# Halves of the output projection between the values products of the last eight heads: an order forced on TensorE, and a left operand split in its own place

## The chip, the cores and the metric

The kernel runs on one core of one Trainium2 chip. The metric is the device time of one execution in microseconds (us). The engines are named as in the profile: PE is TensorE (matmuls; PEld are its weight loads), DVE is VectorE, ACT is ScalarE, POOL is GpSimd, SP is SyncE, whose queue issues every DMA of this kernel, in order.

## What is computed

The reference is one transformer block with 2048 tokens of 1024 channels: a modulated layer norm, attention over 32 heads of 32 channels in four segments of 512 tokens, with a memory that is carried from segment to segment, and an MLP over the token axis. What the change touches is the end of the attention and what follows it:

```python
o = concat over heads and segments of  g * a_mem + (1 - g) * softmax(q k^T * scale + mask) v
x = x + ga * (o @ wo)                              # the output projection
h = _layernorm(x) * (1 + cb) + sb
x = x + gb * _B_ref(h, w1, b1, w2, b2)             # layer norm again, then the token MLP
```

All of it is in float32. Products of float32 are made of parts: an operand is split into a high part and the rest, and three matmuls (high x high, high x rest, rest x high) are summed.

## The kernel before, in words

**Attention.** 32 iterations t run over two passes of two segments each and eight groups of four heads: `its[t] = (pass, group, segment)`. The last two, t = 30 and 31, are group 7 in segments 2 and 3. A head has the number n = 4t + h. The hand-written loop over n (lines 628 to 651) traces the scores of head n, the row maxima of head n + 3, the values of head n - 1, and a quarter of the projections of the iteration two ahead.

- `maxima` (lines 428 to 453): four matmuls into banks s1 (`sx`, `sy`, `sz`), each reduced on DVE with `mask`; for two heads together a transpose (`nmps`) and four small DMAs (`sk<-nt`) that put the negative maxima into the rows of `sk`.
- `scores` (466 to 488): matmuls `a`, exponentials on ACT into `p32`, a triangle cut on POOL (484), a cast on ACT (486), and the rest of the cast in two POOL instructions (488), the last step before the values.
- `values` (490 to 521): 20 matmuls of `ph` and `vp` into the one bank pv (502), then DVE and POOL; after a group's fourth head four transposes (517), a copy and a DMA of 256 KB into `oT` (520).

**Output projection** (`out_proj`, 698 to 749). 16 tiles of 128 tokens, in the order 0, 1, 8, 2, 9, 3, 10, 4, 11, 5, 12, 6, 13, 7, 14, 15. For each tile `oT` is loaded into `otr` (701, one buffer of 512 KB), split by ACT (121) and DVE (124) into `ots` (two buffers), and `x1` is loaded (705, two buffers). Two halves of 512 columns follow, each of 24 matmuls `po` into a bank pj (716; there are two) and a DVE sum with x1 (719). Then x1 is stored (720), and DVE and ACT make the two norms (`modulated`, `normed`). When both tiles k and k + 8 are there, `paired` makes their combinations and, for k under 3, splits seven operands for the MLP (line 124, `bA`); for the others it stores them (745 to 747, `hcd`). The tiles `h2` have three buffers. `wop` are the pages of wo, split long before (593) and loaded (648) into pages that held h for the projections of t = 30 (first half) and t = 31 (second half).

**Memory.** The buffers of the output projection lie where the attention's were: otr and ots on scb, gaw and the raw buffers; x1, h2 and the rest of pool `cw` on `acst` (among it `mask`, `MZ`, `bdg`) and on the weights of the projections.

**The order of the work.** The kernel is traced as one program; a planner then orders each engine's instructions and SP's DMAs by a timeline of its own, with what is traced earlier going first where both are ready. Nothing in the text of the kernel before sets where po stands among the matmuls of the last heads: the planner does.

**The MLP** (`mix`, line 808, `mx`) begins after the last tile's halves and lasts to the end.

Of the kernel before, what the change touches and what calls it, by code (L numbers as in the profile page):

```python
# [7 lines left out]
F32 = mybir.dt.float32  # L8
# [10 lines left out]
P = 128  # L19
# [9 lines left out]
FT = F // P  # L29
LEADP, LEADS, NSK = 8, 3, 8  # L30
XB = 4
NSC = 4
VL = 1
PHB = 2
# [11 lines left out]
def attention_and_mlp(ctx, tc, x, wq, wkv, wo, beta, w1, b1, w2, b2, c, wm_a, wm_b, out):  # L46
# [29 lines left out]
    def bank(tag, bufs, name):  # L76
        return psum.tile([P, 512], F32, tag=tag, bufs=bufs, name=name)
# [39 lines left out]
    def split(dst, src, hi_eng, lo_eng):  # L117

        hi, lo = dst[:, 0], dst[:, 1]
        if hi_eng is A:  # L120
            A.copy(hi, src)  # L121
        else:
            hi_eng.tensor_copy(hi, src)
        lo_eng.tensor_tensor(lo, src, hi.bitcast(F32), op=ALU.subtract)  # L124
# [18 lines left out]
    def new_page(name):  # L143
        return page.tile([P, 2, 512], F32R, tag="page", bufs=16, name=name)
# [345 lines left out]
    def values(t, h):  # L490
        pr, g, seg = its[t]
        d = st[t]
        am, ph = d["am"], d["ph", h]
        pv = bank("pv", 1, f"pv{t}_{h}").rearrange("p (a n) -> p a n", a=4)
        col = {0: lambda i: 128 * i, 1: lambda i: 512 + 128 * (i - 1), 2: lambda i: 1024 + 128 * (i - 2),
               3: lambda i: 896}
        n = 0
        for part, w in ((0, NV), (1, 65)):
            for i in range(4):
                for j in range(i + 1):  # L500
                    o = col[j](i)
                    T.matmul(pv[:, i, 0:w], ph[:, part, o:o + 128], d["vp"][:, j, h, 0:w], start=(n == 0),  # L502
                             stop=(n == 19), skip_group_check=True)
# [12 lines left out]
        for i in range(4):  # L516
            T.transpose(ps[:, 128 * i:128 * i + 128], am[:, i], ident)
# [20 lines left out]
    def mod_rows(lo, hi):  # L538
# [4 lines left out]
        A.copy(row, ps[0:n, 0:128])  # L543
        SY.dma_start(modd.rearrange("a (b n) -> (a b) n", n=P)[lo:hi], row)

    todo = {}

    def plan(n, f, engines=""):
# [79 lines left out]
    for n in range(-LEADS, 4 * NI + VL):  # L628
# [38 lines left out]
    ot_pools = [tc.tile_pool(name=n, bufs=1, reuse_waits="tile") for n in ("otr", "ots")]  # L667
    wr_, ws_ = (q.__enter__() for q in ot_pools)

    gm = {}  # L670

# [22 lines left out]

    bA = [b_tile(b3, 3, q, "bA0") for q in range(NPR)]
    pair_h = {}

    def out_proj(tt):

        r = wr_.tile([P, NK, P], F32, tag="otr", bufs=1, name=f"otr{tt}")  # L700
        SY.dma_start(r, oT[:, :, P * tt:P * tt + P].rearrange("g p n -> p g n"))
# [3 lines left out]
        SY.dma_start(x1, x[P * tt:P * tt + P])  # L705
        h2 = w.tile([P, D], F32, tag="h2", bufs=3, name=f"h2_{tt}")
# [4 lines left out]
        for nh in range(2):  # L711
            ps = bank("pj", 2, f"po{tt}_{nh}")
            n = 0
            for ct in range(NK):
                for i, j in ((0, 0), (0, 1), (1, 0)):
                    T.matmul(ps, os_[:, i, P * ct:P * ct + P], wop[ct, nh][:, j], start=(n == 0), stop=(n == 3 * NK - 1))  # L716
                    n += 1
            c0, c1 = 512 * nh, 512 * nh + 512
            V.tensor_tensor(x1[:, c0:c1], ps, x1[:, c0:c1], op=ALU.add)  # L719
        SY.dma_start(x1d[tt], x1)  # L720

        def modulated():
            mv = ln_stats(w, x1, "b")
# [24 lines left out]

        return modulated, normed, paired

    for tt in [0] + [i for k in range(1, 8) for i in (k, 7 + k)] + [15]:
        rest = out_proj(tt)
        if tt < 15:
            for f in rest:
                f()
    for q in ot_pools[::-1]:
        q.__exit__(None, None, None)
    page_pool.__exit__(None, None, None)
# [253 lines left out]
```

## Time and profile before

| | us |
|---|---|
| three runs | 2292.92, 2293.85, 2296.53 |
| their median | 2293.85 |
| the profiled execution | 2291.74 |
| its span, first to last instruction | 2290.0 |
| PE busy | 2216.0 (97% of the span) |
| DVE busy | 1712.4 (75%) |
| ACT busy | 1110.7 (49%) |
| POOL busy | 738.5 (32%) |

The profiled execution is 1.74 us longer than its span. Its page gives the busy time of each engine, the span in slices, the chain of work that ended last, and groups of instructions; the trace behind it answers for any stretch. Times in the trace count from the span's start: the last projections end at about 983, the first po matmul starts at 984.8, the last values are at 1052.6, the last po matmul at 1206.7, and the MLP takes the rest. Some matmul records can be missing from a trace.

### The profile page before, as it was taken

The page shows a single profiled execution, that of the slowest core. Times are in us where ns is not written, and L with a number is a line of the kernel's source. Part 1 is how long each engine was busy: PE and PEld are TensorE (multiplying, and loading weights), DVE is VectorE, ACT ScalarE, POOL GpSimd, SP SyncE. Part 2 cuts the span into 40 slices and gives each one's busy share as a digit, 9 for nine tenths or more (in the row PEclk, how much of TensorE's full clock was granted, in tenths as well). Part 3 has the DMA queues.
Part 4 walks back from the last instruction along what each step waited for, and adds up shares of the span by engine and source line. Part 5 has one row for each costly group of instructions (what it writes and reads, how often), then busy time and mean ns, then how long its engine had stood idle before and what let it go on. Part 6 is the DMA issues. An engine that isn't in the chain of part 4 may idle for free.

```text
span 2290.0 us, 38358 instructions
## 1 busy us (share of the span) xinstructions
PE 2216.0 (97%) x13802; PEld 1905.0 (83%) x13802; DVE 1712.4 (75%) x3814; ACT 1110.7 (49%) x2026; POOL 738.5 (32%) x843
## 2 busy tenths in 40 slices
PE   7999999998999999999998999999999999999999
PEld 6888898888988889977777888888887888888887
DVE  6686677766776776668888565698889787878787
ACT  6477677665656666654324333443334242424232
POOL 5165666655766766662001000023333000000000
PEclk9999999999999999989999999999999999999999
DMA  6656565687566665664466664566557441414133
GB/s 258 201 169 188 156 195 162 186 283 220 162 196 192 175 199 173 198 204 130 137 215 215 249 234 160 196 229 234 207 202 265 172 152 56 152 56 143 56 120 147
DMA packets 172593, 414.67 MB, mean 181 GB/s; under 512 B 17236, under 2 KB 71540, under 8 KB 163444
## 3 DMA queue, kind: packets, MB, share of 16 engines
q1 hardware_dynamic: 172404, 412.22, 54.7%
q8 instruction: 110, 1.80, 0.3%
q14 instruction: 79, 0.65, 0.1%
HBM read 236.23 MB, written 125.06 MB: 158 GB/s over the span
## 4 chain that ended last, share of the span: by engine, by line
PE 83%; DVE 6%; DMA 4%; ACT 3%; POOL 2%; issue 1%; SPq 0%; DVEq 0%; ACTq 0%; POOLq 0%
PE mx L808 44%; PE nps L194 13%; PE qps L202 8%; PE po L716 5%; PE pv L502 3%; PE a L473 1%; PE sx L438 1%; POOL ph L488 1%; DMA sk<-nt 1%; PE sz L438 1%; PE rd L410 1%; PE a L476 1%; PE up L420 1%; PE a L480 1%; PE sy L438 1%
## 5 line engine op out<-in xcount | busy, mean ns | idle before, releaser
L808 PE MATMUL mx<-bU,sp 128*128 128x512 f32 x2352 | 535.8, 389 | 2.8 <-DVE sp L124 1.7
L808 PEld LDWEIGHTS mx<-bU,sp 128*128 128x128 f32 x2352 | 440.6, 188 | 97.5 <-DVE sp L124 2.7
L194 PE MATMUL nps<-wv,h 128*128 128x256 f32 x3072 | 435.3, 283 | 3.9 <-POOL h L124 3.9
L808 PE MATMUL mx<-bA,sp 128*128 128x512 f32 x1764 | 431.7, 389 | 5.7 <-ACT cc L813 1.9
L488 POOL TENSOR_TENSOR ph<-p,ph 128x640 f16<-128x640 f32 x256 | 379.0, 1502 | 153.2 <-ACT ph L486 153.0
L121 ACT CAST sp<-wr 128x384 fp32r<-128x384 f32 (+2 forms) x408 | 216.8, 545 | 432.5 <-PE mx L808 359.1
L194 PEld LDWEIGHTS nps<-wv,h 128*128 128x128 f32 x3072 | 403.2, 190 | 10.9 <-POOL h L124 5.1
L808 PEld LDWEIGHTS mx<-bA,sp 128*128 128x128 f32 x1764 | 330.6, 188 | 76.3 <-DVE sp L124 2.5
L124 DVE TENSOR_TENSOR sp<-wr,sp 128x384 fp32r<-128x384 f32 (+2 forms) x408 | 258.3, 644 | 38.0 <-ACT sp L121 37.6
L815 DVE TENSOR_TENSOR ac<-mx,ac 128x512 f32<-128x512 f32 x280 | 189.3, 685 | 91.8 <-PE mx L808 91.1
L202 PE MATMUL qps<-h,wq 128*128 128x512 f32 x768 | 197.7, 403 | 2.3 <-DVE pv L505 1.1
L716 PE MATMUL po<-wo,ots 128*128 128x512 f32 x768 | 183.6, 399 | 6.9 <-DVE x L719 5.8
L486 ACT CAST ph<-p 128x1280 f16<-128x1280 f32 x128 | 161.1, 1259 | 47.0 <-POOL p L484 46.3
L716 PEld LDWEIGHTS po<-wo,ots 128*128 128x128 f32 x768 | 147.9, 194 | 38.8 <-ACT mv L133 3.5
L439 DVE CUSTOM_DVE_ANT_0 sx<-sx,mask 128x128 f32<-128x128 f32 (+1 forms) x256 | 110.0, 430 | 88.2 <-PE sx L438 86.6
L202 PEld LDWEIGHTS qps<-h,wq 128*128 128x128 f32 x768 | 142.5, 192 | 31.2 <-issue 2.8
L808 PE MATMUL mx<-bB,sp 128*128 128x512 f32 x588 | 164.4, 389 | 0.0
L484 POOL TENSOR_SCALAR_AFFINE_SELECT p<-p 128x256 f32<-128x256 f32 x256 | 121.3, 483 | 117.2 <-ACT p L477 56.8
L502 PE MATMUL pv<-vp,ph 128*128 128x97 bf16 (+1 forms) x2560 | 145.5, 203 | 4.7 <-DVE mv L135 2.7
L502 PEld LDWEIGHTS <-ph 128*128 128x128 f16 x2560 | 116.6, 99 | 28.8 <-issue 14.8
L815 DVE TENSOR_TENSOR cc<-mx,cc 128x512 f32<-128x512 f32 x140 | 94.5, 682 | 49.3 <-PE mx L808 45.3
L808 PEld LDWEIGHTS mx<-bB,sp 128*128 128x128 f32 x588 | 110.4, 188 | 23.2 <-ACT bB L121 0.3
(177 smaller groups left out, 3204.5 us busy)
## 6 DMA issues: line engine op xcount, KB each, us to landing
sk<-sg SPq DMA_DIRECT2D x384, 128.0 KB
wr<-in_w_dram SPq DMA_DIRECT2D x28, 1024.0 KB
wr<-in_w_dram SPq DMA_DIRECT2D x32, 768.0 KB
bstu<-ucd SPq DMA_DIRECT2D x28, 768.0 KB
wsp<-wv SPq DMA_DIRECT2D x32, 512.0 KB
rawm<-in_wm_b_dram SPq DMA_DIRECT2D x32, 512.0 KB
wv<-wsp SPq DMA_DIRECT2D x32, 512.0 KB
pcd<-cc SPq DMA_DIRECT2D x14, 1024.0 KB
```

The lines of the kernel that those rows point to most:

```text
L121: A.copy(hi, src)
L124: lo_eng.tensor_tensor(lo, src, hi.bitcast(F32), op=ALU.subtract)
L194: T.matmul(ps[:, aa], h[:, j, 128 * tt:128 * tt + 128], wt[:, i, o:o + 256], start=(n == 0), stop=(n >= 6 * NK - 2), skip_group_check=True)
L202: T.matmul(ps, wt[:, i, o:o + 128], h[:, j], start=(k + n == 0), stop=(3 * k + n == 3 * NK - 1))
L439: marks[4 * t + h - LEADS, "V"] = V.tensor_tensor_reduce(o, o, mask[:, 384 - 128 * i:], 1.0, -3.0e38, op0=ALU.add, op1=ALU.max, accum_out= ...
L484: G.affine_select(w, w, pattern=[[0, 2], [1, 128]], compare_op=ALU.is_ge, fill=0.0, base=0, channel_multiplier=-1)
L486: marks[n, "A"] = A.copy(ph[:, 0], p32)
L488: marks[n, "G"] = G.tensor_tensor(ph[:, 1, c], p32[:, c], ph[:, 0, c], op=ALU.subtract)
L502: T.matmul(pv[:, i, 0:w], ph[:, part, o:o + 128], d["vp"][:, j, h, 0:w], start=(n == 0), stop=(n == 19), skip_group_check=True)
L716: T.matmul(ps, os_[:, i, P * ct:P * ct + P], wop[ct, nh][:, j], start=(n == 0), stop=(n == 3 * NK - 1))
L808: T.matmul(ps, ops[q][:, i, P * k:P * k + P], b[:, j], start=(m == 0 and first), stop=(m == 3 * nk - 1), skip_group_check=True)
L815: V.tensor_tensor(d, ps, d, op=ALU.add)
```

## The change

- The eight halves of tiles 0, 1, 2 and 8 are put between the values of the last heads by an explicit order on PE: before the values of head n, and behind those of head n - 1, stands one whole half, for n = 120 to 127: (0,0), (1,0), (0,1), (1,1), (2,0), (2,1), (8,0), (8,1), as (tile, half). The order adds no semaphore; it only binds the planner.
- Tiles 0 and 1 are traced together: first halves, then second halves. The order of the tiles becomes 0, 1, 2, 8, 3, 9, 4, 10, 11, 5, 12, 6, 13, 7, 14, 15.
- `otr` goes. The load from oT writes the second part of `ots`; ACT casts it into the first, and DVE subtracts in place. The room of otr holds tile 2's `h2`.
- The requests for the pages of wo are traced four at a time, at n = 115 and 116 (first half) and 119 and 120 (second half), in place of two at each n from 115 to 122.
- The store of x1 and the tile h2 move behind both halves (`norms`).

```diff
+WOP = {115: (0, 0), 116: (0, 4), 119: (1, 0), 120: (1, 4)}
+FILL = tuple(zip(range(120, 128), ((0, 0), (1, 0), (0, 1), (1, 1), (2, 0), (2, 1), (8, 0), (8, 1))))
...
-        if 4 * NI - 5 <= m < 4 * NI + 3:
-            i = m - 4 * NI + 5
-            for c in (2 * (i % 4), 2 * (i % 4) + 1):
-                wop[c, i // 4] = new_page(f"wo{c}_{i // 4}")
-                SY.dma_start(wop[c, i // 4].bitcast(F32), wos[c, i // 4])
+        if n in WOP:
+            nh, c0 = WOP[n]
+            for c in range(c0, c0 + 4):
+                wop[c, nh] = new_page(f"wo{c}_{nh}")
+                SY.dma_start(wop[c, nh].bitcast(F32), wos[c, nh])
...
+    def left_operand(tt):
+
         os_ = ws_.tile([P, 2, D], F32R, tag="ots", bufs=2, name=f"ots{tt}")
-        split(os_, r.rearrange("p a b -> p (a b)"), A, V)
+        r = os_[:, 1].bitcast(F32)
+        SY.dma_start(r.rearrange("p (a b) -> p a b", a=NK), oT[:, :, P * tt:P * tt + P].rearrange("g p n -> p g n"))
+        A.copy(os_[:, 0], r)
+        V.tensor_tensor(os_[:, 1], r, os_[:, 0].bitcast(F32), op=ALU.subtract)
         x1 = w.tile([P, D], F32, tag="x1", bufs=2, name=f"x1_{tt}")
         SY.dma_start(x1, x[P * tt:P * tt + P])
+        return os_, x1
+
+    def half_proj(tt, nh, os_, x1):
+        ps = bank("pj", 2, f"po{tt}_{nh}")
...
+                mm = T.matmul(ps, os_[:, i, P * ct:P * ct + P], wop[ct, nh][:, j], start=(n == 0), stop=(n == 3 * NK - 1))
+                po_mm.setdefault((tt, nh), []).append(mm.ins)
...
+        V.tensor_tensor(x1[:, c], ps, x1[:, c], op=ALU.add)
+
+    def norms(tt, x1):
+
+        SY.dma_start(x1d[tt], x1)
+        pool, tag, bufs = (ws_, "h2", 1) if tt == 2 else (w, "h2", 3)
+        h2 = pool.tile([P, D], F32, tag=tag, bufs=bufs, name=f"h2_{tt}")
...
+    def out_proj(tiles):
+        ops = [left_operand(tt) for tt in tiles]
+        for nh in range(2):
+            for tt, op in zip(tiles, ops):
+                half_proj(tt, nh, *op)
+        return [norms(tt, x1) for tt, (_, x1) in zip(tiles, ops)]
+
+    for tiles in (0, 1), (2,), (8,), (3,), (9,), (4,), (10,), (11,), (5,), (12,), (6,), (13,), (7,), (14,), (15,):
+        for rest in out_proj(tiles):
+            if tiles != (15,):
+                for f in rest:
+                    f()
+    order = mybir.DependencyInfo(mybir.DependencyClass.NoSync, mybir.DependencyReason.DATA)
+    for n, (tt, nh) in FILL:
+        tc.add_manual_dep(po_mm[tt, nh][0], pv_mm[n - 1][-1].name, order, reason="fills")
+        tc.add_manual_dep(pv_mm[n][0], po_mm[tt, nh][-1].name, order, reason="fills")
```

`pv_mm` and `po_mm` are lists of the values' and the projection's matmuls, kept for this order.

More of the change, by code (lines that the diff above doesn't have):

```diff
@@ L501, in values @@
                     o = col[j](i)
-                    T.matmul(pv[:, i, 0:w], ph[:, part, o:o + 128], d["vp"][:, j, h, 0:w], start=(n == 0),
-                             stop=(n == 19), skip_group_check=True)
+                    mm = T.matmul(pv[:, i, 0:w], ph[:, part, o:o + 128], d["vp"][:, j, h, 0:w], start=(n == 0),
+                                  stop=(n == 19), skip_group_check=True)
+                    pv_mm.setdefault(4 * t + h, []).append(mm.ins)
                     n += 1
@@ L544, in mod_rows @@
         SY.dma_start(modd.rearrange("a (b n) -> (a b) n", n=P)[lo:hi], row)
+    pv_mm = {}
     todo = {}
@@ L666, in attention_and_mlp @@
     w = cw_pool.__enter__()
-    ot_pools = [tc.tile_pool(name=n, bufs=1, reuse_waits="tile") for n in ("otr", "ots")]
-    wr_, ws_ = (q.__enter__() for q in ot_pools)
+    ot_pools = [tc.tile_pool(name="ots", bufs=1, reuse_waits="tile")]
+    ws_ = ot_pools[0].__enter__()
     gm = {}
@@ L710, in out_proj @@
                 spread(gm[i], i)
[L711 to L720, printed above, removed]
         def modulated():
@@ L749, in out_proj @@
         return modulated, normed, paired
[L751 to L755, printed above, removed]
+    def out_proj(tiles):
[13 more added lines that the diff above has]
+        tc.add_manual_dep(pv_mm[n][0], po_mm[tt, nh][-1].name, order, reason="fills")
     for q in ot_pools[::-1]:
```

10 lines of the change are left out of this document (6 added, 4 removed).

## Prediction

> **What bounds the kernel now.** I read the page's busy table and chain first, then busy time by stretch around the change, then PE in order of time.
>
> ```profile
> PE 2216.0 (97%) x13802; PEld 1905.0 (83%) x13802; DVE 1712.4 (75%) x3814; ACT 1110.7 (49%) x2026; POOL 738.5 (32%) x843
> ...
> PE 83%; DVE 6%; DMA 4%; ACT 3%; POOL 2%; issue 1%; SPq 0%; DVEq 0%; ACTq 0%; POOLq 0%
> ```
>
> TensorE (PE) is the bound, 83% of the chain that ended last, so the change can win only where PE waits or runs slow. A view of stretches gives, after the length, busy us and count of PE, weight loads, DVE, ACT and POOL, then PE's granted clock, DMA share and GB/s:
>
> ```profile
> 984.00:1001.00 17.00, 17.00 (x127) 14.41 (x125) 9.08 (x33) 7.92 (x12) 8.45 (x11) 1.00 0.84 262
> 1001.00:1008.00 7.00, 4.38 (x38) 3.08 (x36) 5.32 (x20) 4.33 (x7) 4.61 (x6) 1.00 0.97 340
> 1008.00:1020.00 12.00, 10.88 (x63) 8.54 (x64) 7.87 (x30) 6.86 (x12) 8.07 (x11) 0.52 0.48 172
> ...
> 1036.00:1042.00 6.00, 2.21 (x34) 1.88 (x31) 3.57 (x10) 2.87 (x7) 4.87 (x5) 0.76 0.56 175
> ...
> 1060.00:1135.00 75.00, 72.50 (x321) 59.67 (x319) 69.07 (x135) 29.61 (x54) 0.00 (x0) 1.00 0.42 136
> 1135.00:1165.00 30.00, 26.73 (x105) 21.60 (x106) 24.55 (x54) 7.49 (x17) 0.00 (x0) 0.90 0.64 213
> ```
>
> The reader sees three things. From 1001 to 1042 PE is short of work or slow: 2.6 us idle, then 12 us at a clock of 0.52 (5.8 us of work lost), later 3.8 us idle. From 1060 to 1135 VectorE (DVE) is busy 69 of 75 us, so in the out-projection's tail a second limit stands close behind PE. From 1135 on come 3.3 us idle and a clock of 0.90. PE in order of time (start, length; n = 4t+h numbers the heads, and a head's values are 20 pv matmuls) shows which heads are covered:
>
> ```profile
> 983.19 0.31 PE L502 MATMUL pv<-vp,ph 128*128 128x97 bf16 x3
> ...
> 991.13 0.73 PE L502 MATMUL pv<-vp,ph 128*128 128x97 bf16 x14
> ...
> 998.38 0.31 PE L502 MATMUL pv<-vp,ph 128*128 128x97 bf16 x3
> 998.52 0.68 PE L410 MATMUL rd<-MZ,pq 128*128 128x132 f32 x4
> ...
> 1006.59 0.51 PE L438 MATMUL sz<-sk 96*128 96x512 f32 x1 [1.96 <-DVE mx L439]
> ...
> 1019.88 5.94 PE L716 MATMUL po<-wo,ots 128*128 128x512 f32 x21
> ...
> 1032.47 0.62 PE L517 MATMUL ops<-ident,am 128*128 128x128 f32 x4
> ...
> 1035.45 0.93 PE L502 MATMUL pv<-vp,ph 128*128 128x97 bf16 x20
> ...
> 1042.00 10.70 PE L716 MATMUL po<-wo,ots 128*128 128x512 f32 x38 [1.08 <-ACT ots L121]
> 1052.55 0.92 PE L502 MATMUL pv<-vp,ph 128*128 128x97 bf16 x20
> ...
> 1059.90 72.60 PE L716 MATMUL po<-wo,ots 128*128 128x512 f32 x319
> ...
> 1208.35 1.25 PE L808 MATMUL mx<-bA,sp 128*128 128x512 f32 x4 [1.30 <-ACT sp L121]
> ```
>
> and the matmuls of line 716 alone by stretch:
>
> ```profile
> 984.00:991.00 7.00, 5.85 (x24) 4.44 (x24) 1.00 1.03 411
> ...
> 1002.00:1036.00 34.00, 12.79 (x48) 9.82 (x48) 0.80 0.44 168
> ...
> 984.00:1059.80 75.80, 42.26 (x161) 32.05 (x161) 0.86 0.54 179
> ```
>
> The last row of the first is the first matmul of the MLP. The three first pv rows are heads 117, 118 and 119. Tile 0's first half (24 from 984 to 991) lies before 118 and its second mostly before 119; heads 120 to 122 have none, because tile 0's sums wait for x1 (below) and so both pj banks stay taken until 1019. From 1019.88 on tile 1 (48 by 1036) and tile 8 fill in; head 127 is the row at 1052.55, behind 134 of the 768. So five and a half halves already stand between these heads: the change moves the cover, it doesn't create it.
>
> **The change part by part.** *The cost of a half.* The row at 1059.90 has 319 matmuls in 72.60 us, 0.2276 us each, so 24 take 5.46 us. The change adds no PE work: 768 po matmuls before and after.
>
> *Two heads lose their cover.* The order now lets tile 0's first half start only behind head 119. Heads 118 and 119 then go at the pace of POOL, whose last step (line 488) ends just ahead of the values:
>
> ```profile
> 987.52 2.79 POOL L488 TENSOR_TENSOR ph<-p,ph 128x640 f16<-128x640 f32 x2 [0.76 <-ACT ph L486]
> ...
> 992.60 2.79 POOL L488 TENSOR_TENSOR ph<-p,ph 128x640 f16<-128x640 f32 x2 [1.37 <-ACT ph L486]
> ```
>
> These belong to heads 118 and 119 and end at 990.31 and 995.39, 5.1 us apart; with 0.93 us of pv (row 1035.45) head 119 ends at 996.3, where before it only began at 998.38. PE is some 3 us earlier there, but has done none of tile 0's 48 matmuls (10.9 us).
>
> *Eight heads get a half each.* A covered step took 7.94 us (983.19 to 991.13) and 7.25 us (991.13 to 998.38), maxima and scores included. After head 122 the maxima are over, so I take 7.3 on the average: 58.4 us, 996.3 to 1054.7, less the pv of head 127 that follows the eighth half: 192 matmuls done at 1053.8. Bounds: 7.0 (5.46 + 0.93 and the scores) to 7.94 each, -2.4 to +5.1.
>
> *The third half waits for a bank.* There are two pj banks, so (0,1) needs the first sum of tile 0 evacuated by DVE, and that needs x1.
>
> ```profile
> 1012.56 0.38 SPq L705 DMA_DIRECT2D x<-in_x_dram  x1
> ...
> 1018.58 0.67 DVE L719 TENSOR_TENSOR x<-po,x 128x512 f32<-128x512 f32 x1
> ```
>
> x1 lies where MZ lay, which the rd matmuls read until 999.2, and it went out on SP's queue only at 1012.56, behind the row vectors of the last maxima; its sum ran 6.0 us later. In the new order (0,1) is due at 996.3 + 2 x 7.3 = 1010.9. No half stands before heads 118 and 119 any more, so the maxima come some us earlier and x1 with them. The wait is 0 to 8.4 us (x1's sum as late as 1019.3); I take 3. Queued behind it on PE are heads 122 to 127, by the forced order.
>
> *The clock.* From 1001 to 1008 PE was busy 4.38 of 7 us, no wait longer than the 1.96 us in the row at 1006.59, and 12 us at 0.52 followed. Heads 118 and 119 without cover keep PE about half busy, 984 to 996, so a slow stretch may follow here too: 0 to 5.8 us, but while it lasts PE reaches the bank wait later, and the two overlap. Together with the wait I take 4 us, bounds 0 to 13. The Trainium skill, "TensorE: Matmul & The Clock Gate", section "Why this matters for your kernels", would have the clock fall only after idle gaps of over about 3 us; by that rule the uncovered heads cost no clock, and the 4 us would be 3. The row at 1006.59 speaks against the rule: the clock fell after gaps of 2 us at most.
>
> *Tile 8's halves* come last, behind tile 2's, and need oT of segment 2, whose last transposes ran at 1032.47; before, their left operand held PE until 1042.00. Tile 2 now covers that: nothing is added. The earlier requests for wo pages cost nothing: pages come free with the h pages, whose users have not moved.
>
> *Sum at 192 matmuls.* 1053.8 + 4 = 1057.8. Before: 161 were done by 1059.80 (row of 984 to 1059.80), and 31 x 0.2276 more, from 1059.90 on, end at 1067.0. The lead is 9 us, bounds -6 to +15.5.
>
> *The left operand in place.* The load of tile i+2 now waits for PE's last matmul of tile i, where a spare tile (otr) was loaded ahead. Issue, landing and the two steps of the split:
>
> ```profile
> 1036.10 0.37 SPq L701 DMA_DIRECT2D otr<-oT  x1
> ...
> 1151.41 1.15 SPq L701 DMA_DIRECT2D otr<-oT  x1
> ```
>
> ```profile
> 1040.90 1.04 ACT L121 CAST ots<-otr 128x1024 fp32r<-128x1024 f32 x1 [3.10 <-DMA otr<-oT]
> ...
> 1159.53 1.04 ACT L121 CAST ots<-otr 128x1024 fp32r<-128x1024 f32 x1 [10.75 <-DMA otr<-oT]
> ```
>
> ```profile
> L121 ACT CAST ots<-otr x16: 1044/1056/1056, 942.1 to 1185.3; 128x1024 fp32r<-128x1024 f32 x16
> L124 DVE TENSOR_TENSOR ots<-otr,ots x16: 1206/1218/1226, 943.2 to 1186.4; 128x1024 fp32r<-128x1024 f32 x16
> ```
>
> A quiet load took 4.8 us from issue to use, the one among hcd's stores 8.1. With 1.06 + 1.22 us of split and one DVE instruction of 1.3 us in front the chain is 8.4 to 11.7 us; tile i+1 covers 48 x 0.2276 = 10.9. So quiet tiles are hidden and the four or five beside hcd's stores stand 0.8 us late, 3 to 4 us in all if none has other slack; half of that may fall into the waits that are there already. I take 2.5. If the cover is gone at every tile, the twelve tiles left cost 20 us (rival three); below nothing, the 3.3 us idle after 1135 could vanish. What is behind the load on SP's queue are stores of x1d and loads of x1, which are due later; behind the split on DVE is everything.
>
> *DVE.* The same instructions in number: the copies and the subtraction of the split are only written out. The new tile order has norms of tile 2 done early and the seven splits of pair (0, 8) late: no change of the sum.
>
> **Total.** -9 + 2.5 = -6.5 us, all of it taken from the profiled execution of 2291.74 us (span 2290.0 and 1.74 around it): 2285.2. That execution lies 2.11 us under the median 2293.85; with the median the forecast is 2287.3, so **2287**.
>
> **Rivals.** One: *the bank wait eats the lead.* If x1's sum stays at 1018.6 or slips behind the halves in PE's order, (0,1) starts 8 us late, heads 122 to 127 with it, and the clock falls as at 1008 (5.8 us). The lead, 13 without the 4, is then about -0.6, and with the tail's 2.5 the time is 2297. For it: x1 is issued behind the maxima. Against it: the maxima lose two halves in front of them.
>
> Two: *more is won.* No bank wait, no slow clock, 7.0 us a step: a lead of 15.5, less 2.5: 2281; with the idle after 1135 gone, 2277. For it: the 7.87 us of DVE work in 1008 to 1020 leave room to evacuate. Against it: DVE's 69 of 75 us later.
>
> Three, on the slow side: *the left operand sets the tail's pace.* Its place is the load behind PE's last matmul. From a landing of about 8.2 us on the average (8.2 + 1.06 + 1.22 + 1.3 = 11.8, 0.85 over the cover, twelve times) the lead is gone; at 9 us each tile loses 1.6 us, 20 in all: 2293.85 - 9 + 20 = 2305. For it: the row of 8.1 us, DVE's queue, which stands while a split waits, and DVE is near its limit. Against it: the quiet row of 4.8.
>
> Four: the order isn't kept, or PE's order comes out as before: 2294.
>
> **Chances.** Forecast 0.48 (2282 to 2291), more 0.15, bank wait 0.14, left operand 0.19, not done 0.04. A measurement of this kernel can tell about 0.2%, 4.6 us, from no change: faster is below 2289.3. Of the forecast 0.42 lies there, and all of rival two: faster 0.57. Within 0.2%: 0.06 of the forecast, 0.10 of rival one and 0.04 of four: 0.20. Slower: 0.19 of rival three and 0.04 of rival one, if both its prices fall full: 0.23. The range 2277 to 2301 leaves out the worse half of rival three and little else.
>
> **What would show it.** Right: heads 118 and 119 with pv about 5 us apart and none of po between them; then steps of 7 to 8 us up to head 127; PE idle before po of (0,1) put down to DVE x; the 192nd po matmul about 9 us earlier, near 1058; the tail from there to the first mx within 3 us of the 141.4 us before (1067.0 to 1208.35). Wrong: PE waits on ACT or DVE ots at many tiles in the tail; a gap of over 8 us before (0,1); a clock near 0.5 for over 10 us after 1000; a tail shorter than 139 us.

## The result, and the profile after

The changed kernel takes **2308.93 us** (median of five, 2305.24 to 2311.14) against 2296.53 for the kernel before on the same chip (five, 2292.92 to 2301.19): ratio **1.0053**, 95% interval 1.0042 to 1.0063, 12.2 us slower where 6.5 faster was forecast.

The profiled execution after took 2308.93 us, span 2307.1. Its page, busy times and chain:

```profile
PE 2224.4 (96%) x13802; PEld 1909.5 (83%) x13802; DVE 1712.4 (74%) x3814; ACT 1112.3 (48%) x2026; POOL 741.3 (32%) x843
...
PE 83%; DVE 6%; DMA 3%; ACT 3%; POOL 2%; issue 1%; SPq 0%; DVEq 0%; ACTq 0%; POOLq 0%
```

The same instructions, the same share of PE on the chain: what was lost is waiting and clock, not work. **Where** it was lost is read from a common point. PE's order is the same in both kernels up to the last projection of t = 29, and the end of that projection (A) is at 927.8 before and 933.5 after. No edit of PE's order lies ahead of it, and over the 20 profiles of this study it falls between 927.8 and 935.5, so 5.7 us of the 17.1 us between the two spans are no effect that I can put down to the change. From A on (the 192nd matmul by its start, to some 0.2 us):

| us | before | after | difference |
|---|---|---|---|
| A to the 192nd po matmul | 139.2 | 143.2 | +4.0 |
| from there to the first mx | 141.3 | 146.0 | +4.7 |
| first mx to the end | 1081.7 | 1084.4 | +2.7 |
| A to the end | 1362.2 | 1373.6 | +11.4 |

The lead of 9 us did not come, and the tail grew. PE in order of time after (start, length), heads 119 to 127, two stretches:

```profile
1004.09 0.61 PE L412 MATMUL rd<-MZ,pq 128*128 128x132 f32 x4
...
1004.73 0.36 PE L504 MATMUL pv<-vp,ph 128*128 128x65 bf16 x6
1004.92 2.54 PE L719 MATMUL po<-wo,ots 128*128 128x512 f32 x10
...
1011.13 0.91 PE L504 MATMUL pv<-vp,ph 128*128 128x97 bf16 x20
1012.38 4.29 PE L719 MATMUL po<-wo,ots 128*128 128x512 f32 x18
1016.50 0.60 PE L520 MATMUL ops<-ident,am 128*128 128x128 f32 x4
...
1019.64 0.38 PE L504 MATMUL pv<-vp,ph 128*128 128x65 bf16 x7
1027.21 0.47 PE L481 MATMUL a<-sk 98*128 98x128 f32 x1 [1.96 <-ACT p L476]
1028.28 6.32 PE L719 MATMUL po<-wo,ots 128*128 128x512 f32 x21
...
1035.32 0.91 PE L504 MATMUL pv<-vp,ph 128*128 128x97 bf16 x20
...
1042.08 0.92 PE L504 MATMUL pv<-vp,ph 128*128 128x97 bf16 x20
...
1049.98 0.65 PE L520 MATMUL ops<-ident,am 128*128 128x128 f32 x4
1050.47 0.32 PE L504 MATMUL pv<-vp,ph 128*128 128x65 bf16 x5
...
1056.43 0.92 PE L504 MATMUL pv<-vp,ph 128*128 128x97 bf16 x20
1060.48 0.74 PE L719 MATMUL po<-wo,ots 128*128 128x512 f32 x2 [3.12 <-ACT ots L708]
1062.51 8.19 PE L719 MATMUL po<-wo,ots 128*128 128x512 f32 x22 [1.30 <-DVE ots L709]
1070.55 0.91 PE L504 MATMUL pv<-vp,ph 128*128 128x97 bf16 x20
...
1077.55 0.92 PE L504 MATMUL pv<-vp,ph 128*128 128x97 bf16 x20
```

The order is kept: a half in front of each pv from 120 on. From one pv's end to the next the eight steps take 7.0, 8.0, **16.2**, 6.8, 7.8, 6.6, **14.1** and 7.0 us. Six are what was forecast (7.3); two are not, those with (0,1) and (8,0). SP's queue shows the first (start, length of the issue):

```profile
1010.92 2.56 SPq L454 DMA_DIRECT2D sk<-nt  x4
1017.75 0.33 SPq L523 DMA_DIRECT2D oT<-ot  x1
1020.33 2.49 SPq L454 DMA_DIRECT2D sk<-nt  x4
1022.92 0.85 SPq L711 DMA_DIRECT2D x<-in_x_dram  x2
```

x1 (line 711) stands behind the row maxima of the last heads and a store of oT. The store needs the transposes of t = 29 (the ops row at 1016.50), the maxima need their own matmuls on PE, and all of these now stand behind whole halves. So x1 goes out at 1022.92, 10.4 us later than before, though its own place had been free for 18 us: the last rd, which reads MZ there, ends at 1004.70 (first row above). Its sum, which frees the bank, is on DVE at

```profile
1026.70 0.69 DVE L723 TENSOR_TENSOR x<-po,x 128x512 f32<-128x512 f32 x1 [0.84 <-DMA x<-in_x_dram]
```

and (0,1) starts at 1028.28, 8.3 us behind head 121. The Trainium skill, "DMA: Bandwidth & Descriptors", section "Anatomy of one DMA — SWDGE (gpsimd) path", says that a semaphore wait happens on the issuing sequencer before the dispatch. That section is about DMAs that GpSimd issues, and these are SP's; the rows agree all the same: x1's own place was free, and it still went out only when those in front of it had gone.

How much of the long step is this wait is another question: where x1 comes early (run 3 below), the step is nearly as long.

The second step, (8,0): the transposes of t = 30 (row at 1049.98) come behind half (2,0), the store of oT and the left operand's load follow,

```profile
1052.85 0.32 SPq L523 DMA_DIRECT2D oT<-ot  x1
1055.23 1.76 SPq L707 DMA_DIRECT2D ots<-oT  x2
```

and PE stands 3.12 and 1.30 us. A slow stretch follows. The view of stretches (length; busy us and count of PE, PEld, DVE, ACT, POOL; granted clock; DMA share; GB/s):

```profile
...
1060.50:1070.50 10.00, 8.70 (x24) 6.42 (x24) 8.24 (x14) 3.12 (x7) 5.29 (x3) 0.66 0.32 108
1070.50:1154.50 84.00, 84.00 (x405) 69.27 (x404) 72.10 (x141) 30.98 (x57) 0.91 (x2) 1.00 0.38 123
```

The clock is 0.66 on the average while (8,0) runs: 22 matmuls take 8.19 us, where 5.0 would do (22 x 0.2276). In the tail PE is busy without a break from 1070.5 to 1154.5 and then stops for 7.3 us; one more stop, of 2.2 us, follows at 1199.67. Before, the tail had these two stops:

```profile
1135.18 23.38 PE L716 MATMUL po<-wo,ots 128*128 128x512 f32 x96 [2.68 <-DVE x L719]
...
1161.66 45.40 PE L716 MATMUL po<-wo,ots 128*128 128x512 f32 x192 [3.09 <-DVE x L719]
```

After, PE, SP's queue and DVE around the stop:

```profile
1161.84 35.65 PE L719 MATMUL po<-wo,ots 128*128 128x512 f32 x144 [7.28 <-ACT mv L135]
```

```profile
1154.64 0.37 SPq L707 DMA_DIRECT2D ots<-oT  x1
1155.43 0.33 SPq L711 DMA_DIRECT2D x<-in_x_dram  x1
```

```profile
1153.32 1.28 DVE L737 SCALAR_TENSOR_TENSOR h<-x,mv,gm 128x1024 f32<-128x1024 f32 x1
...
1159.79 1.22 DVE L709 TENSOR_TENSOR ots<-ots 128x1024 fp32r<-128x1024 f32 x1 [0.89 <-ACT ots L708]
...
1161.06 1.23 DVE L723 TENSOR_TENSOR x<-po,x 128x512 f32<-128x512 f32 x2
```

The left operand's load goes out when PE has finished with its place (1154.56). x1 has two buffers, and its load waits for DVE's norm of the tile two before, which reads the buffer last (line 737, to 1154.60); the operand's load in front of it on SP adds at most 0.8 us. The two sums that would free the banks stand behind the split on DVE. PE waits for all of it: load, cast, split, sums. (The row names ACT's mv, which ended last; in runs 2 and 17 below the same stop is put down to DVE x, the sum.)

### The profile page after: what moved, and what is told of

It is laid out like the page before. It is cut to its first block, busy times and chain, and to the rows that moved or that the text cites. A ratio compares the mean times of both kernels' runs of the same rounds, so it can differ in the third digit from the quotient of the medians.

```text
span 2307.1 us, 38339 instructions
## 1 busy us (share of the span) xinstructions
PE 2224.4 (96%) x13802; PEld 1909.5 (83%) x13802; DVE 1712.4 (74%) x3814; ACT 1112.3 (48%) x2026; POOL 741.3 (32%) x843
## 4 chain that ended last, share of the span: by engine, by line
PE 83%; DVE 6%; DMA 3%; ACT 3%; POOL 2%; issue 1%; SPq 0%; DVEq 0%; ACTq 0%; POOLq 0%
PE mx L832 44%; PE nps L196 12%; PE qps L204 8%; PE po L719 6%; PE pv L504 3%; DMA sk<-nt 1%; PE a L475 1%; PE sx L440 1%; POOL ph L490 1%; PE sz L440 1%; PE rd L412 1%; PE a L478 1%; DMA ots<-oT 1%; PE up L422 1%; PE a L482 1%
## 5 line engine op out<-in xcount | busy, mean ns | idle before, releaser
L719 PEld LDWEIGHTS po<-wo,ots 128*128 128x128 f32 x768 | 148.3, 195 | 46.4 <-ACT mv L135 10.2
```

Of the source, the lines that this page charges most:

```text
L719: mm = T.matmul(ps, os_[:, i, P * ct:P * ct + P], wop[ct, nh][:, j], start=(n == 0), stop=(n == 3 * NK - 1))
```

## The experiments

Theory when they began: the change loses by **x1's late load** behind the order, and by the **left operand in its place**. Rivals: the order as such, the lost cover of heads 118 and 119, tile 8's operand, and the order of tiles and norms in the tail. The runs are numbered in the order in which they were made. All ratios are to the kernel before, timed beside each run on the same chip. The last three columns are from one profile each: the sum is from A to the end, less the 1362.2 us of before; it agrees with the timed runs within 5 us but for run 13 (6 us), so single profiles are read no finer than that.

| run | left operand | order | x1 | other | ratio, 95% | A to 192nd | to first mx | sum |
|---|---|---|---|---|---|---|---|---|
| after | in place | yes | late | | 1.0053 (1.0042, 1.0063) | 143.2 | 146.0 | +11.4 |
| 1 | in place | no | late | | 1.0048 (1.0032, 1.0065) | 140.3 | 150.7 | +14.2 |
| 2 | in place | no | late | rest as before | 1.0028 (1.0018, 1.0038) | 146.4 | 145.8 | +9.0 |
| 3 | in place | yes | early | | 1.0000 (0.9987, 1.0012) | 140.7 | 145.0 | +3.2 |
| 4 | in place | other heads | late | | 1.0048 (1.0031, 1.0066) | 140.1 | 148.5 | +13.5 |
| 5 | spare tile | no | early | rest as before | 1.0011 (1.0002, 1.0020) | 146.4 | 136.6 | +1.9 |
| 6 | in place | no | early | | 1.0067 (1.0054, 1.0081) | 145.2 | 147.8 | +18.0 |
| 7 | in place | no | late | as before, third x1 | 1.0008 (0.9998, 1.0018) | 144.8 | 134.0 | +1.4 |
| 8 | in place | six halves | early | | 1.0016 (1.0007, 1.0025) | 137.6 | 148.6 | +5.0 |
| 9 | in place | yes | early | norms, third x1 | 1.0013 (1.0003, 1.0022) | 137.8 | 141.2 | +2.5 |
| 10 | spare tile | yes | early | norms | 0.9997 (0.9986, 1.0008) | 137.3 | 145.5 | -0.3 |
| 11 | in place | no | early | norms, third x1 | 1.0042 (1.0029, 1.0056) | 143.7 | 146.1 | +12.6 |
| 12 | in place | other heads | early | norms, third x1 | 1.0016 (1.0006, 1.0025) | 137.6 | 143.1 | +4.7 |
| 13 | spare tile | yes | late | norms | 1.0011 (1.0001, 1.0021) | 140.4 | 150.0 | +8.6 |
| 14 | spare tile | no | early | norms | 1.0005 (0.9996, 1.0013) | 137.4 | 147.2 | +2.3 |
| 15 | spare tile | no | late | norms | 0.9987 (0.9978, 0.9997) | 134.3 | 148.8 | +0.6 |
| 16 | in place | yes | late | norms | 1.0048 (1.0030, 1.0065) | 144.5 | 152.2 | +13.7 |
| 17 | in place | yes | early | norms | 1.0041 (1.0025, 1.0056) | 139.5 | 153.7 | +11.2 |
| 18 | in place | no | late | norms | 1.0038 (1.0023, 1.0053) | 139.1 | 156.1 | +13.5 |

(x1 "early" is the edit of run 3; "other heads" is that of run 4; "norms" is tile 2's norms behind tile 8's and the rest of the tiles in the order of before.) Where two runs are compared, the difference is that of their ratios times 2296.5 us, with the root of the summed squares of their half intervals.

**Run 1, the order left out.**

```diff
-    for n, (tt, nh) in FILL:
-        tc.add_manual_dep(po_mm[tt, nh][0], pv_mm[n - 1][-1].name, order, reason="fills")
-        tc.add_manual_dep(pv_mm[n][0], po_mm[tt, nh][-1].name, order, reason="fills")
```

> The changed kernel without its forced order: the two orders per half between po and pv are taken out, all else (left operand in place, tile order, tile 2's own h2, requests for wo pages) stays. Theory A (the forced order makes PE stand still: about 8 us before half (0,1) for x1, and about 8 us at tile 8 for its left operand; the left operand in place costs the tail only a few us): with the order gone heads 122 to 127 no longer stand behind (0,1), the time comes back to +1 to +5 us of the kernel before. Theory B (the left operand in place is the cost, through the tail): the time stays within 3 us of the changed kernel, +9 to +15 us of the kernel before.

Measured 2308.12: 1.1 +- 4.5 us from the changed kernel. The written order by itself neither won nor lost; 11 us of loss are there without it.

**Run 2, the in-place left operand alone**, put into the kernel before; otr's 4 KB per partition stay empty.

```diff
-        r = wr_.tile([P, NK, P], F32, tag="otr", bufs=1, name=f"otr{tt}")
+        r = os_[:, 1].bitcast(F32)
...
-        split(os_, r.rearrange("p a b -> p (a b)"), A, V)
+        A.copy(os_[:, 0], r)
+        V.tensor_tensor(os_[:, 1], r, os_[:, 0].bitcast(F32), op=ALU.subtract)
```

> The kernel before with only the left operand's load and split changed: oT is loaded into the second part of ots and split there, otr is gone (its room stays empty), order of tiles and of PE are the planner's as before. Theory A: +1 to +5 us of the kernel before, from loads that wait for PE's last matmul of a tile. Theory B: +9 us or more, ACT and DVE waiting for DMA ots at most of the tail's tiles.

Measured 2303.07, +6.4 +- 2.3 us. Its tail, PE in order of time, has the same stop as the changed kernel's:

```profile
1148.76 23.67 PE L718 MATMUL po<-wo,ots 128*128 128x512 f32 x96 [7.45 <-DVE x L721]
```

Half of the loss comes from this edit with no other part of the change beside it.

**Run 3, x1 early.** `mask`, which the maxima read to the last, lies in another pool, so that x1's pool no longer shares its room; the planner then asks for x1 at 1008.23, ahead of the last maxima.

```diff
-    mask = acst.tile([P, L], BF16, name="mask")
+    mask = top.tile([P, L], BF16, name="mask")
```

> The changed kernel with mask in another pool (top in place of acst), so that x1's memory comes free with the rd matmuls of the last iteration and the planner puts x1's loads on SP's queue before the row vectors of the last maxima. The forced order stays. Theory A: the wait of about 8 us before half (0,1) is gone, heads 122 to 127 move up with it, and the time falls by 6 to 10 us from the changed kernel, to between +2 and +6 us of the kernel before; the wait for tile 8's left operand stays. Theory B: within 3 us of the changed kernel.

Measured 2295.30, 1.0000: **12.2 +- 3.8 us** come back. The stand in front of (0,1) is gone: x1's sum runs at 1014.83, and (0,1) starts at 1023.17, right behind head 121. But the 192nd matmul gains only 2.5 us in the profile. In the changed kernel head 122's scores ran ahead of the half, at 1018.57, while PE waited; now the planner has them behind it:

```profile
1028.89 0.40 PE L475 MATMUL a<-sk 98*128 98x512 f32 x1
```

Its values then wait for POOL until 1037.55, in a slow stretch (rows in the last section), and the step still takes 15.0 us against 16.2. It takes 15.0 to 15.6 in every run with x1 early and the whole order (3, 9, 10 and 17). So the bank's wait doesn't explain the 12 us; what else it moved was to be seen.

**Run 4, cover for heads 118 and 119**: the first two halves stand before them, none before 120 and 121.

```diff
-FILL = tuple(zip(range(120, 128), ((0, 0), (1, 0), (0, 1), (1, 1), (2, 0), (2, 1), (8, 0), (8, 1))))
+FILL = tuple(zip((118, 119, 122, 123, 124, 125, 126, 127), ((0, 0), (1, 0), (0, 1), (1, 1), (2, 0), (2, 1), (8, 0), (8, 1))))
```

> The changed kernel with its first two halves forced before heads 118 and 119, as the planner had them in the kernel before, and none before heads 120 and 121; (0,1) and the five others stay before heads 122 to 127. If the two heads that lost their cover cost what I put down for them (10.9 us of matmuls not done against 3 us gained), the time falls by 5 to 8 us from the changed kernel. Theory A, in which what counts is when x1 lands and when tile 8's operand is there, expects less: heads 120 and 121 lose their cover in its place, half (0,1) still waits for x1, and the time falls by 0 to 4 us, as far as x1 is issued earlier because the maxima have no half in front.

Measured 2307.22, within 0.05% of the changed kernel: the lost cover is not the cause. **Run 12** made the same edit to run 9, with x1 early:

> The third-buffer version with the first two halves put behind heads 117 and 118 again, as in run four, and none behind 119 and 120. Theory A (with x1 on time the lost cover of heads 118 and 119 shows, and the clock of 0.53 after it): 2 to 5 us under the third-buffer version. Theory B (heads 120 and 121 then lose theirs instead): within 0.1% of it, or above.

Measured 2299.55, 0.03% above run 9: the same answer.

**Runs 5 and 6: x1 early without the order**: run 3's edit in the kernel before and in run 1.

> The kernel before with one thing changed: mask lies in the pool that lives to the end, so that x1's place is free earlier and its loads go out earlier on SP's queue; left operand with its spare tile, order as before. Theory A (x1's late load costs by itself, in every order): ratio 0.995 to 0.999, some 2 to 12 us faster, x1 issued before 1008, no stretch without po between tile 0's second half and tile 1's first. Theory B (x1's load was late before too, but only the order written out by hand made it cost, because po of (0,1) is asked for early): ratio 0.999 to 1.001.

> The kernel after without the order written out by hand, with x1's early load: the fourth corner of order by x1. With x1 late the order made 0.0 us of difference (2308.9 and 2308.1). Theory A (the order is worth nothing either way, the early load is worth 12 us): 2295 to 2298, ratio 0.999 to 1.001. Theory B (with x1 on time the order pays as the prediction meant, the early load alone pays less): 2301 to 2306, ratio 1.002 to 1.005.

Measured 2296.87 (+2.5 +- 2.1) and 2311.29 (4.4 +- 4.9 above run 1). Early x1 wins nothing without the order; with it, 12.2 in the pair above. Between runs 6 and 3 the order is worth 15.4 +- 4.2 us. The parts act together, and the price of one cannot be read from one pair.

**Run 7, a third x1 buffer** in the 4 KB that run 2 left empty.

```diff
-        x1 = w.tile([P, D], F32, tag="x1", bufs=2, name=f"x1_{tt}")
+        nth[0] += 1
+        pool, bufs = (ws_, 1) if nth[0] % 3 == 0 else (w, 2)
+        x1 = pool.tile([P, D], F32, tag="x1", bufs=bufs, name=f"x1_{tt}")
```

> The in-place left operand on the order before, as in the second run (2303.1, 1.0028), and a third buffer for x1 in the 4 KB that the spare tile left. Theory A (the stop of 7.4 us in the tail is x1's load, late because it waits for a store and stands behind the load of the left operand, so that DVE's sums come late): stop under 4 us, ratio 0.999 to 1.001. Theory B (the stop is the load of the left operand itself, which may be issued only behind PE's last matmul of the tile two before, and DVE's queue stands behind its split): a stop of 6 to 8 us stays, ratio 1.002 to 1.004.

Measured 2297.03, 1.0008: 4.6 +- 3.2 us of run 2's 6.4 are back. PE in order of time has no stop in that stretch, 372 matmuls in a row:

```profile
1089.70 84.48 PE L720 MATMUL po<-wo,ots 128*128 128x512 f32 x372
```

and DVE shows why:

```profile
1142.66 0.68 DVE L723 TENSOR_TENSOR x<-po,x 128x512 f32<-128x512 f32 x1
1146.96 1.21 DVE L705 TENSOR_TENSOR ots<-ots 128x1024 fp32r<-128x1024 f32 x1
1148.20 0.64 DVE L723 TENSOR_TENSOR x<-po,x 128x512 f32<-128x512 f32 x1
```

Its x1 no longer waits for the norm of the tile two before: it is asked for at 1124.59, where run 2 asked for it at 1141.84. So the first sum runs ahead of the split and frees a bank. The load of the left operand is as late as in run 2 (the split is at 1146.96 here, 1146.79 there); it costs nothing as long as no sum stands behind it.

**Run 8, only the first six halves bound** (from run 3), for tile 8's operand.

```diff
-    for n, (tt, nh) in FILL:
+    for n, (tt, nh) in FILL[:6]:
```

> The kernel after with x1's early load and only the first six halves in the order written out by hand: tile 8's two halves go where the planner puts them. Theory A (PE stood before po of (8,0) for its operand because the transposes of segment 2 came behind a whole half, 3 us idle and a slow clock after it, some 6 us): 2288 to 2292, ratio 0.996 to 0.998. Theory B (heads 126 and 127 then stand for their p, and the tail is as long): 2294 to 2298, ratio 0.999 to 1.001.

Measured 2299.10, 3.7 +- 3.5 us above run 3: nothing is won. In the one profile of each the 192nd matmul is 3.1 us earlier and the tail 3.6 us longer, which is finer than single profiles are read here.

**Runs 9 to 11: a version meant to beat both.** Run 9 is run 3 with tile 2's norms behind tile 8's, which frees the spare h2 tile's 4 KB for a third x1; run 10 has the spare tile of before there; run 11 is run 9 without the order (run 1's edit). Run 9's diff against run 3, beside the third buffer of run 7:

```diff
-        pool, tag, bufs = (ws_, "h2", 1) if tt == 2 else (w, "h2", 3)
-        h2 = pool.tile([P, D], F32, tag=tag, bufs=bufs, name=f"h2_{tt}")
+        h2 = w.tile([P, D], F32, tag="h2", bufs=3, name=f"h2_{tt}")
...
-    for tiles in (0, 1), (2,), (8,), (3,), (9,), (4,), (10,), (11,), (5,), (12,), (6,), (13,), (7,), (14,), (15,):
...
+    finish(out_proj((0, 1)))
+    op2 = left_operand(2)
+    for nh in range(2):
+        half_proj(2, nh, *op2)
+    finish(out_proj((8,)))
+    finish([norms(2, op2[1])])
+    for tt in (9, 3, 10, 4, 11, 5, 12, 6, 13, 7, 14):
+        finish(out_proj((tt,)))
...
```

> The kernel after with x1's early load (run three, 1.0000) and, in the tail, the order of tiles of before (tile 2's norms behind tile 8's), which frees the fourth h2 tile: its 4 KB become a third x1 buffer. Theory A (the gain of the order, 14 us once x1 is on time, is there, and what still hides it is the stop of 7.3 us in the tail, which a third x1 buffer took away in the kernel before): 2288 to 2292, ratio 0.997 to 0.9985, no stop over 4 us in the tail. Theory B (the tail is bound by DVE, so the stop only moves): 2294 to 2298, ratio 0.9995 to 1.001.

> As the run before it, but the 4 KB hold the spare tile of before (left operand loaded ahead, not in its place) and x1 has two buffers. Theory A (what the in-place left operand costs is the order of load, split and sum on DVE and SP, which either the spare tile or a third x1 buffer mends): within 0.1% of the third-buffer version, 2288 to 2292. Theory B (only x1's third buffer mends it): 2294 to 2298 with a stop of 6 us or more in the tail.

> The third-buffer version without the order written out by hand. Theory A (the order is worth some 14 us when x1 comes on time, as runs three and six showed): 2300 to 2306, ratio 1.002 to 1.005. Theory B (the 14 us were the tail's: a poor order of the tail in run six): within 0.1% of the version with the order.

Measured 2298.71, 2294.99 and 2303.28. None of the three beats the kernel before beyond its interval. Run 9's tail still has stops of 4.4 and 2.4 us. Near 1146 run 10 has a stop of 2.1 us where run 17, the same kernel in place, has 7.3 (below). The order is worth 6.7 +- 3.8 us here (11 to 9), not 15.

**Runs 13 to 15: order and x1 with the spare tile**: run 10 with x1 late (13), without the order (14), and both (15). The diff of run 13; 14 leaves out the three lines of run 1.

```diff
-    mask = top.tile([P, L], BF16, name="mask")
+    mask = acst.tile([P, L], BF16, name="mask")
```

> The version with the spare tile, the order of tiles of before in the tail and the order written out by hand (run ten, 0.9997), with x1's load late again as in the changed kernel. Left operand and tail are those of before, so only the order and x1 are left. Theory A (x1's late load costs some 12 us wherever po of (0,1) is asked for by the order): ratio 1.004 to 1.006, 2305 to 2310, a stop without po of 7 us or more before (0,1). Theory B (the 12 us of run three were in part the tail's, by chance of its order): 0.9995 to 1.002.

> Run ten without the order written out by hand, x1 early. Theory A (the order is worth 5 to 15 us when x1 comes on time): ratio 1.002 to 1.006. Theory B (without the in-place left operand the planner's own order is as good, as in the kernel before with x1 early, 1.0011): 0.9995 to 1.0015.

> Run ten without the order and with x1 late: of the change only the halves of tiles 0 and 1 taken in turn and the earlier requests for the wo pages are left. Theory A (these two cost next to nothing, as the prediction said of the wo pages; the changed kernel without its order, 1.0048, owes its loss to the in-place left operand and the norms' order): 0.999 to 1.001. Theory B (taking tiles 0 and 1 in turn delays tile 0's norms and with them the tail): 1.002 to 1.004.

Measured 2299.18, 2297.69 and 2294.41. With the spare tile all four corners lie between 0.9987 and 1.0011; run 15 is the only kernel here whose interval lies below 1, by 3.0 us, less than the 0.2% that I called measurable. The late load behind the order (10 to 13) costs 3.2 +- 3.4 us, not 12; with x1 late the order costs 5.5 +- 3.2 (15 to 13). The first theory, x1's late load, falls by its size: it is not the main loss.

**Runs 16 to 18: the left operand in its place again**, run 2's edit, with nothing else changed against 13, 10 and 15; the 4 KB stay empty.

> The changed kernel with one thing undone, the order of the norms: tile 2's norms behind tile 8's, as before (the spare h2 tile, no longer needed, leaves 4 KB empty). x1 late, order written out by hand, left operand in its place: against run thirteen (spare tile, 1.0011) only the left operand differs, against the changed kernel (1.0053) only the norms' order. Theory A (the in-place left operand is most of the loss, some 9 us): 1.004 to 1.006. Theory B (the order of tiles and norms in the tail is): 1.0005 to 1.002.

> As the run before it with x1 early. Against run ten (spare tile, 0.9997) only the left operand differs, against run three (1.0000) only the norms' order, against run nine (third x1 buffer, 1.0013) only that buffer. Theory A (x1's early load mends what the in-place left operand costs, as run three seems to say): 0.999 to 1.001. Theory B (run three owes its time to the norms' order of the changed kernel, in which the late sums of the tail fall elsewhere): 1.002 to 1.005.

> As run sixteen without the order written out by hand. Against run fifteen (spare tile, 0.9987) only the left operand differs, against run one (1.0048) only the norms' order. Theory A (in place costs 6 to 9 us by itself, as run two showed with 6.4): 1.001 to 1.003. Theory B (norms' order): within 0.1% of run fifteen.

Measured 2307.61, 2305.19 and 2304.42. The same edit, three times alone: **+8.5 +- 4.6 (13 to 16), +10.1 +- 4.4 (10 to 17), +11.7 +- 4.1 us (15 to 18)**, beside run 2's +6.4. And 16 is 1.1 +- 4.7 us from the changed kernel, so with x1 late the norms' order makes no difference that these runs can tell. PE of run 10, then of run 17, at the same place:

```profile
1146.34 67.15 PE L718 MATMUL po<-wo,ots 128*128 128x512 f32 x288 [2.10 <-DVE x L722]
```

```profile
1151.02 46.23 PE L719 MATMUL po<-wo,ots 128*128 128x512 f32 x192 [7.28 <-DVE x L723]
```

SP's queue and DVE there, run 10:

```profile
1137.12 0.37 SPq L706 DMA_DIRECT2D otr<-oT  x1
1141.32 0.33 SPq L710 DMA_DIRECT2D x<-in_x_dram  x1
```

```profile
1145.52 1.27 DVE L722 TENSOR_TENSOR x<-po,x 128x512 f32<-128x512 f32 x2
1146.71 1.22 DVE L126 TENSOR_TENSOR ots<-otr,ots 128x1024 fp32r<-128x1024 f32 x1
```

and run 17:

```profile
1143.81 0.37 SPq L707 DMA_DIRECT2D ots<-oT  x1
1144.27 0.53 SPq L711 DMA_DIRECT2D x<-in_x_dram  x1
```

```profile
1149.05 1.23 DVE L709 TENSOR_TENSOR ots<-ots 128x1024 fp32r<-128x1024 f32 x1 [0.92 <-ACT ots L708]
1150.19 1.28 DVE L723 TENSOR_TENSOR x<-po,x 128x512 f32<-128x512 f32 x2
```

In both kernels PE ends a tile near 1144 (1097.34 + 46.90 in run 10, 1098.46 + 45.28 in run 17) and needs a sum, and the sum needs x1. The load of x1 waits for the norm that reads its buffer last, in run 10 and in run 17:

```profile
1140.02 1.27 DVE L735 SCALAR_TENSOR_TENSOR h<-x,mv,gm 128x1024 f32<-128x1024 f32 x1
```

```profile
1142.44 1.28 DVE L736 SCALAR_TENSOR_TENSOR h<-x,mv,gm 128x1024 f32<-128x1024 f32 x1
```

With the spare tile the operand had been asked for at 1137.12; the norm ends at 1141.29, x1 goes out at 1141.32, and the sums run ahead of the split. In place, the operand's load can go only at 1143.81; the norm ends at 1143.72, x1 goes out at 1144.27 behind that load, and the sums stand behind the split. So x1 is 2.95 us later, 2.4 of them because DVE is later and some 0.5 by SP's queue, and the place behind the split does the rest of the 5.2 us at this stop. The two other pairs have 2.7 against 7.2 us (13 and 16) and 2.4 against 5.1 (15 and 18) there.

DVE shows the common cause. Between 1076 and 1165 it stands for ACT's casts of the left operand for 4.0, 3.9 and 5.9 us in runs 17, 16 and 18, and for 0.4, 0 and 0.3 us in runs 10, 13 and 15. In run 7 it stands for them too (5.2 us) and PE has no stop: what costs is that the sums stand behind. That DVE is 2.4 us later in run 17 fits these waits; it was not shown by itself. Both kernels also have a stop near 1098, of 5.3 and 5.5 us, which is not the operand's.

## Why the prediction was wrong, step by step

- **"The left operand in place", 2.5 us: the step that failed most.** Measured 6.4 by itself and 8.5 to 11.7 beside the other edits, so most of the 12.2 (8.5 +- 4.6 in the pair nearest to the changed kernel, 13 to 16). Rival three had the place (the load behind PE's last matmul of the tile, DVE's queue behind the split) and its range of up to 20 us held the cost, but I gave it 0.19. The size was wrong because I set the chain against PE's cover, 48 matmuls, as if only the next split could be late. I wrote that "behind the split on DVE is everything" and put no price on it, and this is the term that failed. DVE stands 3.5 to 5.9 us for the casts in the tail (runs 2, 16, 17 and 18; 4.4 in the changed kernel) where the kernel before and its like stand 0 to 0.4; the sums that free PE's banks stand behind the split, and x1 comes later because its buffer waits for DVE. On SP's queue x1's load did stand behind the operand's, but that was 0.8 us at most in the changed kernel. By single profiles part of the cost lies ahead of the tail too: the 192nd matmul is 2.2 to 4.8 us later in place (10 to 17, 13 to 16, 15 to 18).
- **"The third half waits for a bank", 3 us of 0 to 8.4.** It was 8.3, as late as the bound. I had x1 come earlier because the maxima would; they came behind the halves, and x1, behind them on SP, 10.4 us later. The mechanism was named, its direction was wrong. And the wait was not the whole of that step: without it (run 3) the step with (0,1) takes 15.0 us instead of 16.2, because head 122's scores then stand behind the half.
- **"Tile 8's halves ... nothing is added"** failed: 4.4 us of waits and a clock of 0.66. One half covers the operand, not two, since the transposes of t = 30 themselves stand behind half (2,0). With x1 early this step takes 8.4 to 8.7 us (runs 3, 9, 10 and 17); why was not settled.
- **"Eight covered steps of 7.3 us"** held for the six steps without these waits (6.6 to 8.0, mean 7.2). The two others took 30.3 us where 14.6 were meant: 15.7 us, of which the sum had 4.
- **"Heads 118 and 119 lose cover"**: head 119's values end 71.6 us after A, forecast 68.5. The slow stretch that the prediction held possible came, a clock of 0.51 from 997 to 1004. Putting the cover back (runs 4 and 12) gained nothing.
- **The lead of 9 us** was -4.0. Taken apart: 3.1 from the start and 15.0 from the eight steps (73.4 against 58.4), less the 4 in the sum, make 14.1; the 192nd matmul came 13.2 after its forecast. Even with PE's waits for the bank and for tile 8 gone (run 10: spare tile, early x1) the profile shows a lead of 1.9 us, as head 122's step still takes 15.6, and the order wins 1.8 +- 3.2 us there against run 14; where it won more (6.7 and 15.4 us), it was against orders of the planner that were slow themselves (runs 11 and 6). So the plan had little to win: before, five and a half of the eight halves were between these heads already, which the prediction says and still booked 9 us for. (Its lower bound, -6, adds the wait and the clock in full, 14.2 us; with the 13 that it states the bound is -4.9. The -4.0 lies inside both.)
- **"The earlier requests for wo pages cost nothing"** fits run 15, where they and tiles 0 and 1 in turn are what is left, with the norms' order of before: 0.9987.
- **DVE no change, PE no change**: held (1712.4 us of DVE in both).

What stays **open**: with the norms' order of the changed kernel, early x1 returned 12.2 us (run 3), with that of before 1.6 +- 5.4 (16 to 17); between runs 3 and 17 only the norms' order differs, and it makes 9.4 +- 4.6 us. Run 3 is in place and has the stop of 7.3 us, yet loses nothing as a whole; run 8, also in place, has no stop over 2.7 us in its tail. So the one stop is not the whole account, and what an edit costs here depends on the order of the rest. Run 17's tail has a stop of 5.5 us near 1098 besides that of 7.3, run 3's has only the latter; but of these two the changed kernel has only the latter too. Its profile pays later, with a PE wait of 2.4 us for the MLP's second operands and 1084.4 us from the first mx to the end, where run 3 has 1079.6. Why the early load moves that was not settled.

## What to carry to other kernels

A tile that is saved by loading in place ties its load to the last reader of the place; look not only at whether the load still fits under the cover, but at what stands behind its first consumers on their engines, and whether one of those frees what the bottleneck needs next. An order forced on one engine also orders, through the queues, whatever waits for that engine's results: follow each DMA that stands in front of the load you count on. And before filling gaps by hand, subtract the cover that is there already, and ask what stands in line behind the wait that is to go.

## What the runs showed of the hardware

The granted clock fell after short waits again. In run 3 PE has no gap for 19.9 us, then is thinly busy for 3.9 us with no wait over 0.38, and the clock falls to half (length, busy us and count of PE, granted clock, DMA share, GB/s):

```profile
1009.40:1029.30 19.90, 19.90 (x128) 1.00 0.69 264
1029.30:1033.20 3.90, 2.96 (x13) 1.00 0.66 209
1033.20:1043.40 10.20, 7.73 (x34) 0.50 0.21 78
```

The longest wait of that time, 1.46 us, comes when the clock is down already, and the half behind it runs 19 matmuls in 7.20 us, 0.379 each against 0.2276:

```profile
1037.55 0.51 PE L504 MATMUL pv<-vp,ph 128*128 128x65 bf16 x6 [1.46 <-POOL ph L490]
1037.87 7.20 PE L719 MATMUL po<-wo,ots 128*128 128x512 f32 x19
```

From 1029.3 on scores and values waited in turn for ACT and POOL. The Trainium skill, "TensorE: Matmul & The Clock Gate", section "Why this matters for your kernels", ties the loss to idle gaps of over about 3 us; the stretch at (8,0) of the changed kernel, with a gap of 3.12, agrees, and this one does not. The 10.2 us at half the clock are some 5 us of lost work, in the very step whose wait run 3 took away.
